# A fused attention and Fourier-mixing kernel on one core: the hand-played order of its first part is replaced, omega's load changes its queue, and the weight loads wait for the first values

## The chip, the cores and the metric

The kernel runs on one core of a Trainium2 chip. A core has TensorE (PE, with its weight loads shown apart as PEld), VectorE (DVE), ScalarE (ACT), GpSimd (POOL) and SyncE (SP); each works through its own instructions in order, and waits on semaphores for the others. The metric is device time in microseconds (us), the median of repeated runs. The profile is of one execution; its times count from the span's start.

## The reference

Two blocks follow each other. The first is attention with random features: batch 8, 8 heads, sequence 576, head size 64, 128 features.

```python
def phi(x):                              # x is q or k, scaled by 64 ** -0.25
    h = x @ omega.T - sum(x * x) / 2
    return exp(h - max(h)) / sqrt(128)
kv, z = phi(k).T @ v, sum(phi(k))        # per batch and head
x = (phi(q) @ kv) / (phi(q) @ z + 1e-6)  # heads side by side: [8, 576, 512]
```

The second mixes with a Fourier transform and ends in a two-layer perceptron:

```python
u = x + real(fft(fft(x, axis=1), axis=2))
un = (u - mean(u)) / sqrt(var(u) + 1e-6)
out = u + max(un @ w_ch1, 0) @ w_ch2     # 512 -> 2048 -> 512
```

The weights w_ch1 and w_ch2 arrive as 64-bit floats; the kernel reads them as pairs of 32-bit words and makes 32-bit floats of them itself.

## The kernel before

**Two parts.** The first part holds all attention, all mixing, the conversion and preparation of the weights, and four "plain" tiles of 128 rows of the perceptron. The second part does the other 4096 rows in eight blocks of 512, with a Strassen-like scheme (lines 1118 on, 1309). Both are written as generators, the streams, that yield a `Step` (engine or engines, length in us, latency, events it waits for, buffers it takes and gives) ahead of the instructions that the step stands for. `Listing` (line 107) plays them against a planner's clock, and the instructions come out in that order, in one queue for each engine.

**What sets the order.** In the second part, `run` always takes the step that can start first. In the first part it doesn't choose: the string `PICKS` (line 48) holds one character for each of its 1819 steps, the place in the list of waiting steps, in base 36. So in the first part the planner's lengths don't set the order. They still set which engine does a step that names two, and which PSUM bank is taken. The constants RATE, HOP and TURN (lines 38 to 41) are the planner's DMA rate, the delay from one engine to another, and the cost of a change of matmul shape.

**The first part, pair by pair.** There are 32 pairs of heads (`attn`, line 512), handled by three streams in turn. For one pair:

- SP loads k and q (lines 347, 350; 288 KB each; two buffers) and v (line 355; three buffers, vd).
- PE transposes k and q in nine 128x128 blocks (line 470), ACT evicts them (line 477, kqT).
- PE makes the scores against omega (line 544, 64x64 corners of the array), DVE takes the maximum of each group (line 488, nmx), ACT makes the exponentials (line 505, e).
- PE sums keys times values (line 578), ACT or DVE keeps the result (lines 592, 594), PE transposes the query features (line 470) and makes numerators and denominators (lines 621, 629). DVE divides (lines 638 to 641) into x.

After four pairs a batch is whole, and `mix` (line 653) follows: DVE and POOL fold x (lines 668 to 694), PE multiplies with cosine and sine tables (lines 712, 739, 744), ACT keeps and DVE and POOL add up (lines 760 to 778), SP stores u to memory.

**The weights.** `weights` (line 422) issues 32 loads of 512 KB on POOL's queue (line 434, raw), with four buffers; each is followed by `narrow` (line 397): a multiplication on ACT or POOL (lines 409, 407), four instructions on DVE (lines 411, 413, 416, 418), and an addition on POOL (line 420). The plain tiles need the converted weights: line 863 transposes a normed tile, line 924 multiplies with w1, line 947 with w2. `w2_parts` (line 998), `weight_sums` (line 1062) and `block_norms` (line 976) prepare the second part.

**The start.** omega (om) is loaded by two DMAs on SP's queue (line 366) ahead of everything else there; PE transposes it (line 449) and DVE scales it (line 451) before the first scores. Each stream of the list waits for events: `weights` begins when the planner has issued the load of vd number 1, an event of the planner alone, with no instruction behind it.

Of the kernel before, what the change touches and what calls it, by code (L numbers as in the profile page):

```python
# [3 lines left out]

# [12 lines left out]
F32 = mybir.dt.float32  # L17
# [20 lines left out]
RATE = 190.0  # L38
HOP = 0.15

TURN = 0.1
# [7 lines left out]
    "00e2ede0ebed3dedebfcdcddfeede3fdfhbi8cdefdebfdgafaggec9hddk0kiij2jejgj7lfffffhcdfffdfcggjehegfi7gjbl"  # L49
    "hbhkjgkkdihfhi7hci7bfiadgkhhjce9didbhhb7gggbfihbbf97acbhbeghefaie8bc7chhhcgfc7cedddh9dd1ccdfif8eggih"  # L50
    "f6g8ejihichdihidfkhfhgjckgigh6eihggiddebd6dcg9eei7cfhei6ddfgihhj78gmkmiidaggjfigdmlg6khhjcj6agghifgg"
    "kh6afejekjkjfigji6j8hjjjiilcj9iegcigdhllkmldjmkkf9j80lca5m7bdai6gfikjaljkika6lhjggic9feikeejhgjij5d7"
    "ldjeafedkdeikjje5g5ielfafej6egkicg8dffgikghjijiee7eeifaaeefhefehdeh7iffd6hb7eeidiedhggiijbkj35fjkjhk"
    "kfgfhkk3h795g4e4i6khchlijigkjji4hlfjfd8lfhlg4mi64bfgjjedjgibk6ijj5cgcijhicgi6lii9fi9lf6ggdijf6bgd8fe"
    "icddchifajihj9fgihgjgi6jbhi6degcbg48ffgfh6ii5kjigihf7jgf9ejggafji7gf7egdfh6ficd6dbhfeeh5addfh5be5bff"
    "c48gai8hg9ageefcj5j7gh6haeeghhjikiehi5mg6lghhl5jjhagd5nglkmlccnjldj9llj45lkjjaemh6gbmlf8f7hgekef6hke"
    "87cldljj8bkhihbhhdc6ffgadkdf7ad5kdbgjhhig6lgcel5mdjedilaidedejihgjegi5ggjhcf5dgc5c775kccdh489j8ddgff"
    "h8cbdgiejkkechjhkkki5gj7kgjjjjfjjjh4i7dhhjjfi4k4h4kjchehg6ihk975g5bfejcehg3dgmggiej6m55bf9igig5h66gg"
    "jjjfiieifh8ege5kdihdlhiheief9k5fimhmcio8hgk7fge5jhgdeifagbgbjeeekhgclgigh7ge8fgefddfaci4icdffhgfid8f"
    "gjffhgihd6gc6cjeelgf3af8hbiccgchgfebg5c9d6ehdfcfeeagghffbhc6f9egchggh6aeehfeekjccbdfafdf50h0gcgabgea"  # L60
    "7fcdcfabg6be8bd4c9dcdcdbcebe6bcgb6cefbacadfeaca7dcdcdchdf9abca66f8dcbd8b98c8aa9c8dd2eabcc87a7b758697"
    "a27277ba9688848aa89a99992b98aa9a287a888729d8a993ba8ac9788aede65bdaacb69ba8ba659b54387a986aaa9baccade"
    "ad9b7bfcecffffde79fe9e6h9bgc3gc3be1eac26e7ebeddbdfeefegd6cdfed2ddf3dadeb3e3cc9dc6c5dbbdcab7b3c72b79b"
    "acbb8abbb679a6a9bb9ab49c7b38a93caa998888888888899888686981458778888888888888841933648786583b59691776"
    "a7c67267761bb4bcb6cc9a679a8aaba3f94df49cbaa675793a9aa88778388a88a93995aa39b94a4954585536126424112222"
    "3333533555523346545266421330442216087635433437704543770334535754155544556455155414437756241426224444"
    "1112032232202111100"
# [39 lines left out]
class Listing:  # L107
# [4 lines left out]
    def __init__(self, buffers):  # L112
        self.free = dict.fromkeys((PE, ACT, DVE, POOL, SP, NONE, PORT), 0.0)
        self.buffers = {name: [0.0] * n for name, n in buffers.items()}
        self.made = {}
        self.moved = 0.0
        self.mode = "whole"
        self.banks = [0.0] * 8
        self.got = None
# [12 lines left out]
    def start(self, step, ready, before):  # L132

        queued = before in step.engines and len(step.engines) == 1
        t = ready[0] if queued else ready[1]
        for ev in step.after:
            if ev not in self.made:
                return None
            t = max(t, self.made[ev])
        for name in set(step.take):  # L140
            if name in WIDTH:
                t = self.banks_at(WIDTH[name], t)[1]
                if t == math.inf:
                    return None
                continue
            free = sorted(self.buffers[name])
            n = step.take.count(name)
            if len(free) < n:
                return None
            t = max(t, free[n - 1])  # L150

        def begin(e):
            return max(t, self.free[e] if e != NONE else 0.0, self.free[PORT] if step.on_port(e) else 0.0)

        eng = min(step.engines, key=lambda e: begin(e) + step.engines[e])
        t = begin(eng)
        return t + (TURN if eng == PE and step.mode != self.mode else 0.0), eng

    def run(self, streams, picks=None):
        todo = []  # L160
        picks = iter(picks or ())

# [14 lines left out]
        while todo:  # L177
# [20 lines left out]
            done = end + step.late + (HOP if eng != NONE else 0.0)  # L198
            if step.kb:
                self.moved = max(self.moved, end) + step.kb / RATE  # L200
                done = max(done, self.moved + 1.6)
# [52 lines left out]
def kernel(  # L254
# [110 lines left out]
    for i in range(2):  # L365
        nc.sync.dma_start(om[:, i, :], omega[:, :])
# [4 lines left out]
    om2 = fix.tile([128, MF], F32, name="om2")  # L371

# [24 lines left out]
    def narrow(i, dst, raw):  # L397


        lo, hi = raw[:, :, 0], raw[:, :, 1]  # L400
        lof, hif, bits = lo.bitcast(F32), hi.bitcast(F32), dst.bitcast(U32)


        step = Step({ACT: 0.72, POOL: 1.4}, after=(("raw", i),), port=True, bias=1.11)
        yield step
        if step.eng == POOL:
            nc.gpsimd.tensor_scalar(dst, hif, 2.0**-112, None, op0=ALU.mult)
        else:
            nc.scalar.activation(out=dst, in_=hif, func=AF.Copy, scale=2.0**-112)
        yield Step(DVE, 0.43, port=True, bias=0.19)  # L410
        nc.vector.tensor_scalar(hi, hi, 0x80000000, None, op0=ALU.bitwise_and)
        yield Step(DVE, 1.15, port=True, bias=0.36)
        nc.vector.scalar_tensor_tensor(
            bits, bits, 3, hi, op0=ALU.logical_shift_left, op1=ALU.bitwise_or
        )
        nc.vector.tensor_scalar(hi, bits, 0xFF800000, None, op0=ALU.bitwise_and)
        yield Step(DVE, 0.7, port=True, bias=-0.99)
        nc.vector.scalar_tensor_tensor(lof, lo, 2.0**-52, hif, op0=ALU.mult, op1=ALU.mult)  # L418
        yield Step(POOL, 1.3, makes=("w", i), give=("slab",), port=True, bias=1.25)
        nc.gpsimd.tensor_tensor(out=dst, in0=dst, in1=lof, op=ALU.add)  # L420

    def weights():
# [3 lines left out]
        yield Step(NONE, after=(("vd", 1),))  # L426
# [17 lines left out]
    def first():  # L444

        yield Step(NONE, 3.0)
        yield Step(PE, 0.4, take=("bank",))
        b, omps = got()
        nc.tensor.transpose(omps[:, 0:128], om[:].rearrange("m i d -> m (i d)"), ident[:])
        yield Step(DVE, 0.3, makes="om2", give=(b,))  # L450
        nc.vector.tensor_scalar(om2[:], omps[:, 0:128], SCALE, None, op0=ALU.mult)

    def transposed(src, name, groups, after, makes, give, back=None):
# [3 lines left out]
        for j0, j1 in groups:  # L457
# [3 lines left out]
                0.11 * m,  # L461
# [12 lines left out]
    def evicted(dst, b, j0, j1, makes, back):  # L474
        yield Step(ACT, 0.15 + 0.115 * (j1 - j0), 0.1, makes=makes + (j0,), give=(b,), bias=0.08)
# [5 lines left out]
    def softmax(n, ts, num, b, es):  # L481
# [3 lines left out]
        yield Step(DVE, 0.15 + 0.27 * num, bias=-0.56)  # L485
# [10 lines left out]
        for i, one in enumerate(b):  # L496
            if num == 4 or not i:
                yield Step(
                    ACT, 1.18 if num == 4 else 0.65, 0.0, take=(size,),
# [12 lines left out]
    def attn(n):  # L512
# [16 lines left out]
        def pairs_of(js, *ts):  # L529
# [4 lines left out]
                0.235 * len(js),  # L534
# [52 lines left out]
        def keep():  # L587
            step = Step({DVE: 0.3, ACT: 0.35}, take=("kv",), give=(kvb,), makes=("kv", n))
# [20 lines left out]
            1.23,  # L609
# [24 lines left out]
        yield Step(DVE, 1.25, after=(("frame", b),), give=(ndb,), makes=("x", b, pr), bias=-0.07)  # L634
# [18 lines left out]
    def mix(b):  # L653
# [7 lines left out]
        def folds(n):  # L661
            op = (ALU.add, ALU.subtract)[n]
            even, odd = (ALU.subtract, ALU.add) if n else (ALU.add, ALU.subtract)
            step = Step({DVE: 1.22, POOL: 2.5} if n else DVE, 1.22, take=("half",), port=True)
# [4 lines left out]
            yield Step(DVE, 1.15, port=True, bias=-0.08)  # L669
# [3 lines left out]
            for dst, src in ((h[:, 0:NL], h[:, 0:NL]), (h[:, NL : NL + 1], x[:, 4:5])):  # L673
# [7 lines left out]
                {DVE: 1.2, POOL: 2.6} if n else DVE, 1.2,  # L681
# [18 lines left out]
        for n, (tab, name) in enumerate(((cs, "cs"), (cs, "cs"), (sn, "sn"), (sn, "sn"))):  # L700
# [19 lines left out]
            def kept(n=n, yb=yb, yp=yp):  # L720
                yield Step(ACT, 0.44, 0.1, makes=("y", b, n), give=(yb,), bias=0.1)
                nc.scalar.activation(out=y[:, n, :], in_=yp[:, 0:NK], func=AF.Copy)

            yield Fork(kept())
        for c in range(NC3):
# [3 lines left out]
                1.33,  # L729
# [23 lines left out]
    def residual(b, c, x, abb):  # L753
# [3 lines left out]
        yield Step(ACT, 0.4, 0.1, take=("bmp",), give=(b1,))  # L757
# [4 lines left out]
        for last, (dst, op) in enumerate(((mi, ALU.subtract), (pl, ALU.add))):  # L762
            yield Step(DVE, 0.67, give=(b0,) if last else (), bias=-0.1)
# [23 lines left out]
        yield Fork(summed(0, mi, pl, DVE, 0.85))  # L787
        if c < NL:
            yield from summed(1, pl, mi, POOL, 1.6)
# [54 lines left out]
    def norm_of(j, t, i, pool, dst):  # L844
# [7 lines left out]
        yield Step(DVE, 1.09, bias=-0.23)  # L852
# [3 lines left out]
        yield Step(POOL, 0.7, port=True, bias=-0.18)  # L856
        nc.gpsimd.tensor_tensor(rstd[:], rstd[:], mhalf[:], op=ALU.pow)  # L857
        yield Step(DVE, 0.56, port=True)
        nc.vector.tensor_scalar(u[:], u[:], mv[:, 0:1], rstd[:], op0=ALU.subtract, op1=ALU.mult)
        yield Step(PE, 0.45, take=("bank",), give=("u",))  # L860
# [5 lines left out]
        yield Step(ACT, 0.6, 0.1, give=(b,), makes=("unT", j, i), bias=0.33)  # L866
# [25 lines left out]
    def plain_of(j):  # L892
# [4 lines left out]
        def hidden(fc, b, hp):  # L897
            step = Step(
                {ACT: 0.15 + TP / 1130.0, DVE: 0.15 + TP / 945.0},
                late=0.1,  # L900
# [12 lines left out]
        for fc in range(NFC):  # L913
            yield Step(
                PE,
                8 * TP / 1193.0,
# [38 lines left out]
    def rest(t, b, yp):  # L955
# [3 lines left out]
        yield Step(DVE, 0.7, after=(("op", t),), give=(b,), bias=1.38)  # L959
# [16 lines left out]
    def block_norms(j, pool):  # L976
# [13 lines left out]
        for i, (o, l, r, op) in enumerate(ops):  # L990
            yield Step(DVE, 0.7, makes=("tt", j) if i == 3 else None, port=True, bias=-0.49)
# [6 lines left out]
    def w2_parts():  # L998
# [14 lines left out]
        def op(o, l, r, **kw):  # L1013
            step = Step({DVE: 0.7, POOL: 1.35}, port=True, **kw, bias=-0.63)
# [47 lines left out]
    def weight_sums(groups):  # L1062
        yield Step(NONE, after=("converted",))
        for g in groups:
# [6 lines left out]
            for i, (o, l, r, op) in enumerate(ops):  # L1071
                yield Step(DVE, 0.7, makes=("w1s", g) if i == 3 else None, port=True)
# [34 lines left out]
    late = ctx.enter_context(tc.tile_pool(name="late", bufs=1))  # L1107
    listing.buffers = {k: [0.0] * n for k, n in dict(
# [338 lines left out]
```

## Time and profile before

| | us |
|---|---|
| median of five runs | 1225.64 |
| lowest and highest | 1223.47 and 1227.53 |
| the profiled execution, its own time | 1224.47 |
| its span in the profile | 1222.6 |
| PE busy | 1188.5 (97%) |
| PEld busy | 1065.0 (87%) |
| DVE busy | 745.8 (61%) |
| ACT busy | 458.0 (37%) |
| POOL busy | 383.3 (31%) |

The page begins with these busy times, then cuts the span into 40 slices of 30.6 us and gives the busy share of each in tenths. Busy time of PE is modelled from pipelined matmuls, so a busy PE may still issue matmuls further apart than it could; start times of successive matmuls tell more. The chain of work follows the last instruction back to what released it, step by step; each of its rows has a start, a length, an engine, a tile, a line and a number of instructions. A row of waits has the engine that waited, the one it waited for, the total, the number of waits and the longest.

The DMA queues moved 206.02 MB, 169 GB/s over the span; in the first 20 us it was 275 GB/s.

### The profile page before, as it was taken

What the parts mean: (1) busy time and instruction counts of PE and PEld (TensorE: products, weight loads), DVE (VectorE), ACT (ScalarE), POOL (GpSimd) and SP (SyncE); (2) the same over time, 40 slices, a digit from 0 to 9 for tenths busy, and PEclk for the clock granted to TensorE, in tenths of its full rate; (3) what the DMA queues carried; (4) which work ended last, traced back from release to release, by engine and by line L of the source; (5) the groups of instructions that cost most, each with busy time, mean ns of one, the idle gap of its engine ahead of it and who ended that gap; (6) DMA issues with size and microseconds to landing.
All of it is one profiled execution on the core that took longest, in us unless ns stands there. A gap on an engine that the chain in (4) does not pass through costs nothing.

```text
span 1222.6 us, 31614 instructions
## 1 busy us (share of the span) xinstructions
PE 1188.5 (97%) x12705; PEld 1065.0 (87%) x12705; DVE 745.8 (61%) x1522; ACT 458.0 (37%) x1432; POOL 383.3 (31%) x451
## 2 busy tenths in 40 slices
PE   6989889999999999999999999999999999999997
PEld 5778878878878777999899899899899899899897
DVE  4899999896674664384384285285276266267255
ACT  6867767666653521222222222222222222222211
POOL 3443443531111013322422421432431531431421
PEclk9999999999999999999999999999999999999999
DMA  9564654636663334195096096186176276268255
GB/s 262 155 209 143 201 176 145 215 93 201 184 193 130 123 113 163 50 308 169 32 305 190 9 305 190 31 285 191 51 260 199 59 248 219 61 210 256 61 175 171
DMA packets 149058, 206.02 MB, mean 169 GB/s; under 512 B 49328, under 2 KB 62896, under 8 KB 148912
## 3 DMA queue, kind: packets, MB, share of 16 engines
q1 hardware_dynamic: 144224, 187.15, 49.1%
q0 software_dynamic: 4608, 16.78, 4.1%
q8 instruction: 101, 1.65, 0.6%
q14 instruction: 45, 0.37, 0.1%
q10 hardware_dynamic: 80, 0.07, 0.0%
HBM read 172.23 MB, written 35.91 MB: 170 GB/s over the span
## 4 chain that ended last, share of the span: by engine, by line
PE 92%; DVE 4%; ACT 2%; issue 1%; DMA 0%; SPq 0%; DVEq 0%; ACTq 0%
PE banks L1130 32%; PE banks L1309 29%; PE banks L924 5%; PE banks L947 5%; PE banks L470 4%; PE banks L544 4%; PE banks L712 4%; PE banks L578 3%; PE banks L621 2%; PE banks L739 2%; ACT e L505 1%; PE banks L863 1%; DVE nmx L488 1%; PE banks L744 1%; ACT kqT L477 1%
## 5 line engine op out<-in xcount | busy, mean ns | idle before, releaser
L1116 DVE CUSTOM_DVE_ANT_0 hid<-banks,s 128x256 f32<-128x256 f32 x192 | 79.7, 423 | 254.9 <-PE banks L1130 254.9
L1309 PE MATMUL banks<-wl,sums 128*128 128x128 f32 x1792 | 220.2, 275 | 0.0
L1309 PEld LDWEIGHTS banks<-wl,sums 128*128 128x128 f32 x1792 | 210.5, 192 | 1.0
L505 ACT ACTIVATE e<-banks,nmx 128x128 f32<-128x128 f32 x576 | 158.9, 397 | 41.0 <-DVE nmx L488 41.0
L1144 ACT ACTIVATE s<-banks 128x256 f32<-128x256 f32 x192 | 73.6, 383 | 257.6 <-PE banks L1130 257.6
L1130 PE MATMUL banks<-unT,w 128*128 128x256 f32 x704 | 167.3, 379 | 0.0
L1130 PEld LDWEIGHTS banks<-unT,w 128*128 128x128 f32 x704 | 132.7, 190 | 17.9 <-issue 0.5
L1284 ACT ACTIVATE s<-banks 128x128 f32<-128x128 f32 x168 | 46.5, 277 | 236.6 <-PE banks L1309 175.3
L1130 PE MATMUL banks<-tt,w1s 128*128 128x256 f32 x512 | 126.3, 379 | 0.0
L1197 POOL TENSOR_TENSOR hs<-hid 128x256 f32<-128x256 f32 x64 | 46.4, 725 | 200.1 <-DVE hid L1116 173.5
L1130 PEld LDWEIGHTS banks<-tt,w1s 128*128 128x128 f32 x512 | 97.2, 190 | 13.3
L488 DVE TENSOR_REDUCE nmx<-banks 128x8 f32<-128x1024 f32 (+1 forms) x96 | 88.3, 952 | 32.2 <-PE banks L544 27.6
L1309 PE MATMUL banks<-wl,hid 128*128 128x128 f32 x768 | 98.8, 275 | 0.0
L1309 PEld LDWEIGHTS banks<-wl,hid 128*128 128x128 f32 x768 | 94.0, 192 | 1.2
L1289 DVE TENSOR_TENSOR part<-banks,s 128x128 f32<-128x128 f32 x168 | 48.6, 289 | 75.3 <-PE banks L1309 74.2
L1197 POOL TENSOR_TENSOR hs<-hid,hs 128x256 f32<-128x256 f32 x64 | 46.4, 726 | 118.7 <-issue 93.3
L1130 PE MATMUL banks<-unT,w1s 128*128 128x256 f32 x320 | 80.6, 379 | 0.0
L544 PE MATMUL banks<-om,kqT 64*64 64x128 f32 x2304 | 77.0, 276 | 3.4 <-ACT kqT L477 2.0
L857 POOL TENSOR_TENSOR rstd<-rstd,mhalf 128x1 f32<-128x1 f32 x36 | 29.0, 806 | 153.2 <-DVE rstd L855 137.4
L544 PEld LDWEIGHTS banks<-om,kqT 64*64 64x64 f32 x2304 | 64.1, 134 | 14.6 <-ACT kqT L477 4.6
L1309 PE MATMUL banks<-wl,hs 128*128 128x128 f32 x576 | 74.9, 275 | 0.4 <-DVE part L1289 0.4
L420 POOL TENSOR_TENSOR w<-w,raw 128x512 f32<-128x512 f32 x32 | 43.8, 1367 | 99.0 <-DVE raw L418 79.2
(115 smaller groups left out, 1998.6 us busy)
## 6 DMA issues: line engine op xcount, KB each, us to landing
wl<-w2l SPq DMA_DIRECT2D x392, 256.0 KB, 3.6
raw<-in_moe_w_ch_dram POOLq DMA_DIRECT2D x32, 512.0 KB, 5.0
kq<-in_k_dram SPq DMA_DIRECT2D x32, 288.0 KB, 4.4
kq<-in_q_dram SPq DMA_DIRECT2D x32, 288.0 KB, 4.3
vd<-in_v_dram SPq DMA_DIRECT2D x32, 288.0 KB, 4.6
out_dram<-ur SPq DMA_DIRECT2D x68, 128.0 KB, 2.4
u<-us SPq DMA_DIRECT2D x32, 256.0 KB, 4.0
ur<-us SPq DMA_DIRECT2D x32, 256.0 KB, 3.5
```

The source lines that it names most:

```text
L470: nc.tensor.transpose(ps[:, (j - j0) * 128 : (j - j0 + 1) * 128], src(j), ident[:])
L488: nc.vector.tensor_reduce(nmx[:, :, 0:num], pps[:, :, 0 : MF * num].rearrange("p b (c m) -> p b c m", m=MF), axis=AX.X, op=ALU.max, negate ...
L505: nc.scalar.activation(out=e[:, c + (i if num == 1 else 0), :], in_=pps[:, i, MF * c : MF * c + MF], func=AF.Exp, bias=nmx[:, i, c : c + 1],)
L544: nc.tensor.matmul(pps[cols, c, MF * m : MF * m + MF], lhsT=kqT[rows, j, cols], rhs=om2[rows, :],)
L712: nc.tensor.matmul(yp[:, 0:NK], lhsT=fold[:, c, n, :], rhs=tab[:, c, :], start=(c == 0), stop=(c == NC3 - 1),)
L924: nc.tensor.matmul(hp[:, 0:TP], lhsT=w1[:, dc, 128 * fc : 128 * fc + 128], rhs=unTs[key][:, dc, :], start=(dc == 0), stop=(dc == NDC - 1),)
L947: nc.tensor.matmul(yp[:, 0:DM], lhsT=hs[fc][:, 128 * i : 128 * i + 128], rhs=w2[:, fc, :], start=(fc == 0), stop=(fc == NFC - 1),)
L1116: nc.vector._custom_dve(TENSOR_ADD_SAT, out=o, in0=ps, in1=sb, s0=FMAX, s1=0.0)
L1130: nc.tensor.matmul(ps[:, 0:HT], lhsT=left(dc), rhs=right(dc), start=start and dc == 0, stop=(dc == D2 - 1), skip_group_check=True,)
L1144: nc.scalar.activation(out=s[:], in_=ps[:, 0:HT], func=AF.Copy)
L1197: nc.gpsimd.tensor_tensor(out=o, in0=l, in1=r, op=op)
L1309: nc.tensor.matmul(ps[:, 0:128], lhsT=left[:, f], rhs=wls[j, i, n][:, f], start=start and f == 0, stop=(f == 3), skip_group_check=True,)
```

## The change

- **Planner.** The constants move into a tuple `Clock`, one for each part. The first part's clock has another DMA rate and hop, a `lead` ahead of PE's steps, a `tail` of latency for each engine, a `lag` after PE, and a list of engines on which a stream's next step may follow in the queue without waiting for the end. The second part's clock has the old constants, empty tails and lags, and all engines in that list.
- **Step lengths** of the first part are set anew, some 30 of them.
- **PICKS** is replaced as a whole; it has 1819 characters as before.
- **omega** is loaded on ACT's queue instead of SP's.
- **Gate.** `weights` begins with a copy of one element of vd0 on POOL, which waits until v of the first pair has landed; the weight loads stand behind it in POOL's queue.

The diff, cut: of PICKS the first line, of the step lengths those that the text speaks of.

```diff
-RATE = 190.0
-HOP = 0.15
-
-TURN = 0.1
+class Clock(NamedTuple):
+    rate: float
+    hop: float
+    lead: float
+    turn: float
+    tail: dict
+    lag: dict
+    queues: tuple
+
+
+FIRST = Clock(
+    270.0, 0.036, 0.2, 0.12, {PE: 0.163, ACT: 0.105, DVE: 0.085, POOL: 0.02}, {DVE: 0.12, ACT: 0.055},
+    (PE, SP, NONE),
+)
+SECOND = Clock(190.0, 0.15, 0.0, 0.1, {}, {}, (PE, ACT, DVE, POOL, SP, NONE))
...
 PICKS = (
-    "00e2ede0ebed3dedebfcdcddfeede3fdfhbi8cdefdebfdgafaggec9hddk0kiij2jejgj7lfffffhcdfffdfcggjehegfi7gjbl"
...
+    "00ed01eaaeda3eeefbgeddeege9h3hhhhhbggciajkcfdalaabgallekffjkkji3iigeh0iiiidhh7ggggcffdfcffghgbiefhe8"
...
     def __init__(self, buffers):
+        self.clock = FIRST
...
     def start(self, step, ready, before):
 
+        clock = self.clock
         queued = before in step.engines and len(step.engines) == 1
-        t = ready[0] if queued else ready[1]
+        queued = queued and (before in clock.queues or step.kb > 0)
+        t = 0.0 if queued else ready[1]
...
+        if PE in step.engines:
+            t += clock.lead
+        if queued:
+            t = max(t, ready[0])
+
         def begin(e):
-            return max(t, self.free[e] if e != NONE else 0.0, self.free[PORT] if step.on_port(e) else 0.0)
+            u = ready[1] + clock.lag.get(e, 0.0) if before == PE and not queued else 0.0
+            return max(t, u, self.free[e] if e != NONE else 0.0, self.free[PORT] if step.on_port(e) else 0.0)
...
-            done = end + step.late + (HOP if eng != NONE else 0.0)
+            done = end + step.late + clock.tail.get(eng, 0.0) + (clock.hop if eng != NONE else 0.0)
             if step.kb:
-                self.moved = max(self.moved, end) + step.kb / RATE
+                self.moved = max(self.moved, end) + step.kb / clock.rate
...
     for i in range(2):
-        nc.sync.dma_start(om[:, i, :], omega[:, :])
+        nc.scalar.dma_start(om[:, i, :], omega[:, :])
...
+    gate = fix.tile([1, 1], F32, name="gate")
...
-        step = Step({ACT: 0.72, POOL: 1.4}, after=(("raw", i),), port=True, bias=1.11)
+        step = Step({ACT: 0.57, POOL: 1.55}, after=(("raw", i),), port=True, bias=1.11)
...
-        yield Step(DVE, 0.43, port=True, bias=0.19)
+        yield Step(DVE, 0.34, port=True, bias=0.19)
...
-        yield Step(DVE, 1.15, port=True, bias=0.36)
+        yield Step(DVE, 1.19, port=True, bias=0.36)
...
-        yield Step(DVE, 0.7, port=True, bias=-0.99)
+        yield Step(DVE, 0.61, port=True, bias=-0.99)
...
-        yield Step(NONE, after=(("vd", 1),))
+        yield Step(POOL, 0.1, after=(("vd", 0),))
+        nc.gpsimd.tensor_copy(out=gate[:], in_=vds[0][0:1, 0, 0:1])
...
-        yield Step(ACT, 0.15 + 0.115 * (j1 - j0), 0.1, makes=makes + (j0,), give=(b,), bias=0.08)
+        yield Step(ACT, 0.05 + 0.107 * (j1 - j0), 0.02, makes=makes + (j0,), give=(b,), bias=0.08)
...
-        yield Step(DVE, 0.15 + 0.27 * num, bias=-0.56)
+        yield Step(DVE, 0.063 + 0.267 * num, bias=-0.56)
...
-                    ACT, 1.18 if num == 4 else 0.65, 0.0, take=(size,),
+                    ACT, 1.0 if num == 4 else 0.5, 0.04, take=(size,),
...
-            step = Step({DVE: 1.22, POOL: 2.5} if n else DVE, 1.22, take=("half",), port=True)
+            step = Step({DVE: 1.13, POOL: 2.5} if n else DVE, 1.13, take=("half",), port=True)
...
-                {ACT: 0.15 + TP / 1130.0, DVE: 0.15 + TP / 945.0},
-                late=0.1,
+                {ACT: 0.165, DVE: 0.2},
...
     late = ctx.enter_context(tc.tile_pool(name="late", bufs=1))
+    listing.clock = SECOND
```

## The prediction

> **What bounds the kernel now.** I read the page's slices first, then the busy times by stretch, the chain of work, the waits and the groups by shape. The slices (30.6 us each) say where time can be won at all:
>
> ```profile
> PE   6989889999999999999999999999999999999997
> ...
> DVE  4899999896674664384384285285276266267255
> ```
>
> PE is at 9 from the seventh slice on; the low digits are at the left, where DVE stands at 8 and 9. The second part begins at 464.6 us (first matmul of line 1130). In the trace its matmuls follow each other every 216 ns (line 1130) and 112 ns (line 1309), and the 95th percentile of both spacings is the same as the median: nothing to win behind 464.6 us. So the question is the first part. By stretches (PE, PEld, DVE, ACT, POOL busy, clock, DMA):
>
> ```profile
> 0.00:20.00 20.00, 11.01 (x244) 9.52 (x245) 5.61 (x8) 10.46 (x33) 9.23 (x18) 1.00 0.91 275
> 20.00:60.00 40.00, 36.40 (x839) 30.12 (x839) 33.62 (x59) 34.47 (x116) 12.56 (x11) 1.00 0.69 181
> 60.00:100.00 40.00, 34.61 (x850) 31.24 (x850) 35.44 (x70) 28.23 (x89) 18.04 (x19) 0.96 0.66 194
> ...
> 180.00:220.00 40.00, 39.80 (x785) 34.70 (x784) 37.60 (x75) 30.06 (x99) 17.29 (x17) 0.96 0.48 154
> ...
> 300.00:340.00 40.00, 40.00 (x723) 36.23 (x720) 24.76 (x54) 26.83 (x89) 6.98 (x8) 1.00 0.57 166
> ```
>
> To 300 us DVE is busy 85 to 94%, afterwards 62% or less, with PE full. Busy PE is not dense PE, so I price the PE work itself, from rows of the chain where a step is followed at once by the next:
>
> ```profile
> 360.67 3.63 PE banks L947 x8
> ...
> 371.20 7.14 PE banks L924 x64
> 378.35 3.23 PE banks L712 x12
> ...
> 397.20 1.21 PE banks L578 x72
> 398.41 1.97 PE banks L544 x72
> ...
> 418.92 1.08 PE banks L621 x32
> 420.00 0.23 PE banks L629 x8
> ```
>
> Per pair of heads: 1.97 + 1.21 + 1.31 (lines 621, 629) + 18 transposes of line 470 in 2.02 = 6.51; 32 pairs are 208.3 us. Per batch: two line 712 rows, 6.46, and lines 739/744, 4.3; eight are 86. Per plain tile: two 7.14 rows and 32 matmuls of line 947 at 0.43 (the 1.72 us rows of four), 28.0; four are 112. Transposes of line 863: 8 x 0.44 = 3.5. **Floor 410 us, against 464.6**: 54.8 us of loss, of which 11.7 fall into 0 to 20 us, 36.0 into 20 to 240, 3.9 into 240 to 300, 3.2 into 300 to 420 (each stretch's length less the floor of the matmuls in it). In 20 to 240 it is waits on in-order queues; PE's and ACT's (total us, times, longest):
>
> ```profile
> PE banks L470 <- ACT e L505: 5.3, 6, 1.9
> PE banks L578 <- ACT e L505: 2.8, 4, 1.3
> PE banks L621 <- ACT e L505: 2.0, 1, 2.0
> ```
>
> ```profile
> ACT e L505 <- DVE nmx L488: 16.0, 16, 1.9
> ```
>
> PE waits for the exponentials (line 505), which wait for DVE's maxima (line 488), which stand in DVE's queue behind conversions and mixing. The profiled execution took 1224.47 us, 1.87 more than its span and 1.17 under the median 1225.64; I add 1.17 at the end.
>
> **The change, part by part.** 1. *Step lengths.* The picks are played, so the lengths set no order; they set which engine takes a step that allows two (conversion lines 407/409, kv, folds, relu, line 1017) and which PSUM bank. Old against new against the trace: exponentials of four 1.18, 1.0, 1.15 (a chain row of four); eviction of four 0.61, 0.478, 0.61; maxima 1.23, 1.131 plus a tail of 0.085, 1.22. The new lengths are the engine's issue time with the latency split off, and the sum is what the trace shows. One group is planned shorter than it runs: the conversion on DVE, 2.28 before, 2.14 after, against 0.509 + 0.822 + 0.590 + 0.703 = 2.62 in the trace.
>
> 2. *Start.* om's two loads leave SP's queue, so the first k load issues at 0.73 instead of 1.65 us. The four raw loads (2 MB, issued 1.38 to 4.1 us) leave the way of kq and vd. The first transpose now waits for kq until 6.90 us. A kq load lands 4.4 us after issue by the page's median, so 5.1 us; not above 275 GB/s, 288 KB cannot take under 1.1 us, so not before 1.9 us. PE's first step wants om: 4.16 us now; if it queues behind ACT's table load (1.28 us) it lands 1.28 later, 5.4, and its transpose of 0.44 ends at 5.9. Bounds of the gain: 6.90 - 5.9 = 1.0 and 6.90 - 4.6 = 2.3; I take 1.8, nearest to the kq row. PE's first transposes run slowly there (nine in 2.18 us at 6.90, nine in 1.20 at 13.22); that moves along and is neither gain nor loss. Following the first thirty picks by hand, the queue is k, q, vd, then the next k, q, and the gate; PE's first three steps of scores keep their order, so the exponentials hold PE at 9 to 13 us as before: nothing more is booked.
>
> 3. *The gate.* One 1x1 copy on POOL waits for vd0 (now landing 11.2 us after its issue at 3.60). Its own time: between 0.10 (a 128x1 memset) and 0.71 us (line 857's power on 128x1); 0.1 taken, in idle POOL (9.2 of 20 us busy). Behind it on POOL stand all raw loads and line 407. vd0 lands after 4.6 us (page) to 11.2 us from an issue near 1.7, so the first raw load issues at 6.3 to 12.9 instead of 1.38 and lands 5 us later, 11.3 to 17.9; four conversions of 1.53 follow. DVE first touches raw (line 411) at 27.8 us, so 4 to 10 us of cover remain: cost 0. Without that cover it is 32 conversions that start late, but they are spread to 200 us: at most the delay itself, 5 to 11 us, once. SP, moved past by om alone, is free earlier; ACT's queue has two issues of about 0.45 us before its first eviction at 8.05: hidden.
>
> 4. *The order.* Bounds from the stretches. Nothing gained: 0. If 20 to 240 us ran like 240 to 300 (3.9 in 60, 1.3 per 20): 36.0 - 14.3 = 21.7 us. DVE is busy 89% of 20 to 240, and full cover would need 99%, so it can come only by moving DVE work to 300 to 420 us, where DVE is busy 62%. Half, 11, is taken: of the waits above 0.3 us between PE's steps (28 us from 20 us on) a part is of this kind, a part DVE's own load. What is late next is DVE's maxima again, then ACT.
>
> 5. *Second part.* Its clock holds the old constants, and with them each new branch of start() gives the old answer. What differs is only the times at which the first part leaves the engines. The hand-over at 464.6 us has no wait now; DVE is busy 27.4 of the last 44.6 us, so a first part shorter by 13 still fits its weight sums and norms: 0.
>
> Sum: -1.8 - 11 = -12.8; 1224.47 - 12.8 + 1.17 = **1212.8 us**.
>
> [...] The rows say the clock ran at 0.96 in 60 to 100 and in 180 to 220 us: in each, 3.4 us at half speed, 1.7 us of work lost, although no gap between PE's steps there is over 2.6 us. [...] By the rows, dips stand only in the loose stretch, and a denser one could be spared both, 3.4 us; I book none. On om, the rows give 0.92 us of SP time. [...]
>
> **The rivals.**
> - *Start alone* (0.10): the order brings nothing since DVE's 89% is the limit, and one late wait replaces another. 1225.64 - 1.8 = 1223.8, within 0.2%, which is what a measurement of this kernel can tell from no change. For: DVE's digits. Against: DVE has 38% free after 300 us.
> - *More than forecast* (0.15): the whole 21.7, the start's 2.3 and both dips, 27.4: 1198.
> - *Less than forecast* (0.10): the start and 3 us of the order: 1221.
> - *Slower* (0.17): DVE becomes the bound. Its conversions are planned 0.48 us short each, 32 x 0.48 = 15.4 us; with a tighter order these stand before maxima in DVE's queue, in 20 to 240 us, each maximum then holds ACT and PE. It decides once DVE passes about 19 of 20 us there. If PE pays half, and the order gains nothing: +7.7 - 1.8 = +5.9, 1231.5; all of it, 1239. For: POOL and DVE on the conversion slow each other (line 416 takes 0.43 us alone and 1.43 beside line 420 at 77.2 us). Against: the old order carries a shortfall of 0.34 each already.
> - That the change doesn't do what it says is open only for "order kept"; part 5 gives it 0.
>
> **How the numbers follow.** Forecast as worked out 0.48 (1206 to 1220), the rivals 0.15, 0.10 (faster), 0.10 (same), 0.17 (slower). Faster by over 0.2%: 0.48 + 0.15 + 0.10 = 0.73; same 0.10; slower 0.17. The range takes in 1199 (most of the better rival) and 1231 (half of the slower one), leaving out about 2 in 10.
>
> **What would show it.** Right: line 1130 begins at 450 to 455 us; the first transpose at 4.6 to 5.9; raw's first issue between 6 and 13; PE's waits for line 505 in 20 to 240 us halved; DVE over 62% after 300 us; line 1130's spacing still 216 ns. Wrong: DVE over 95% in 20 to 240 us with PE below 36 of 40; the second part longer than 758 us; PE waiting at line 924 for converted weights.

## The result, and the profile after

The changed kernel takes 1228.94 us (median of 25 runs, 1224.96 to 1234.15), the kernel before 1225.57 in the same comparison (49 runs). The ratio is 1.0028 [1.0020, 1.0036]: **slower by 3.4 us**, where 12.8 less was forecast. The profiled execution of the changed kernel took 1229.93 us, with a span of 1228.1. New lines stand about 24 lower in the code: 470 is now 494, 477 501, 488 512, 505 529, 544 568, 578 602, 621 645, 924 947, 1130 1154.

First the timeline of PE in the changed kernel at both ends of the first part (start, duration, instruction, in brackets the idle time before it):

```profile
4.89 0.45 PE L473 MATMUL banks<-ident,om 128*128 128x128 f32 x1 [4.89 <-DMA om<-in_omega_dram]
5.13 2.13 PE L494 MATMUL banks<-ident,kq 128*128 128x128 f32 x9
...
470.20 1.03 PE L1154 MATMUL banks<-unT,w 128*128 128x256 f32 x4
```

The first transpose is 1.77 us earlier (5.13 for 6.90), and yet the second part begins 5.6 us later (470.20 for 464.57). From there to the end it is 757.9 us, before 758.0. So all of the loss lies between 5 and 470 us. The slices and the stretches (columns as before):

```profile
PE   7989989999999999999999999999999999999997
...
DVE  5897978898776433274284285275275266266255
```

```profile
0.00:20.00 20.00, 13.48 (x292) 12.02 (x295) 7.18 (x10) 12.15 (x39) 4.87 (x16) 1.00 0.84 256
20.00:60.00 40.00, 36.32 (x902) 31.57 (x898) 33.22 (x61) 36.26 (x121) 11.96 (x11) 0.96 0.73 205
60.00:100.00 40.00, 34.21 (x739) 30.75 (x732) 34.55 (x67) 28.34 (x93) 16.93 (x18) 0.96 0.60 178
...
180.00:220.00 40.00, 35.53 (x696) 30.80 (x690) 32.93 (x66) 28.65 (x93) 15.27 (x17) 0.96 0.51 151
220.00:260.00 40.00, 38.08 (x863) 32.83 (x854) 35.48 (x68) 32.66 (x110) 13.75 (x13) 0.96 0.63 192
...
300.00:340.00 40.00, 39.28 (x799) 31.80 (x799) 29.16 (x64) 28.11 (x90) 10.40 (x9) 1.00 0.80 252
```

In 180 to 220 us PE is busy 35.5 instead of 39.8, and DVE isn't the reason: it too is less busy, 32.9 for 37.6. Four stretches stand at clock 0.96 instead of two. What PE waits for in 20 to 240 us (us in total, times, longest), and below it ACT:

```profile
PE banks L568 <- issue: 3.5, 2, 2.1
PE banks L494 <- ACT e L529: 3.4, 4, 1.6
PE banks L602 <- issue: 3.2, 3, 2.7
PE banks L494 <- DVE x L665: 2.5, 1, 2.5
PE banks L602 <- ACT e L529: 2.3, 3, 1.3
...
PE banks L645 <- DVE kv L616: 1.8, 1, 1.8
```

```profile
ACT e L529 <- DVE nmx L512: 21.6, 15, 5.7
```

The waits for the exponentials (line 529, before 505) did fall, from 10.5 to 6.1 us, small rows included. Two single waits for DVE came in, 2.5 and 1.8. All rows with a named engine make 16.6 before and 12.9 after: 3.7 won in this stretch. Behind it, from 240 us to the second part, the new order has named waits of 3.2 us, where the kernel before has none; the two largest rows:

```profile
PE banks L736 <- DVE fold L711: 1.6, 1, 1.6
PE banks L494 <- ACT e L529: 1.0, 2, 0.6
```

So over both stretches only some 0.5 us of named waits are won. But 6.7 us now stand at **"issue"** in 20 to 240 us: PE waited for nothing that the profile shows. In the kernel before, this row is missing from 20 to 240 us. The chain of work names the places (start, us, what):

```profile
181.62 1.42 issue
183.03 1.54 PE banks L568 x48
184.57 1.28 PE banks L494 x9
185.85 1.20 PE banks L602 x70
187.06 2.69 issue
189.74 0.33 PE banks L602 x2
```

PE stops after 16 of 64 and after 70 of 72 matmuls of one kind, in the middle of a step, and the profile shows no semaphore that it waits for. Over the whole first part such gaps ("gaps at issue"; here and below those over 0.25 us, from 10 us on) make 6.88 us (at 89.6, 94.7, 183.0, 189.7 and 324.0); before it is one of 0.62. The page's lines on instructions and on DMA queues give a reason to think of:

```profile
PE 1191.3 (97%) x12705; PEld 1069.8 (87%) x12705; DVE 729.0 (59%) x1512; ACT 457.1 (37%) x1445; POOL 370.7 (30%) x449
...
q8 instruction: 101, 1.65, 0.6%
```

Queue q8 carries 101 packets of 16 KB, and PE has 25,410 recorded instructions: 252 to a packet, about 256 with those that its sequencer handles (25,835 in all). So a packet is a block of PE's own program. In the trace the packets that bear on the three large gaps begin at 92.30, 180.58 and 187.31 us; PE goes on at 94.66, 183.03 and 189.74, each time 2.4 us later. Between these points stand 13 times 256 and once 256 instructions: PE goes on with the first one of the block that was fetched. Counted from there, PE had 0, 32 and 0 instructions left when the three packets began. In the kernel before it never had under 59 from 20 us on, and the median packet of either kernel begins with some 190 to 200 left. The packet itself is not slow: 0.95, 0.92 and 0.97 us at the three, 1.0 in the median. It begins late: 2.7, 2.4 and 4.3 us after PE took up the block in hand, against a median of 1.1 in this kernel and 0.8 in the one before. The stretches of these three delays, and the gap behind the third:

```profile
89.56:92.30 2.74, 2.74 (x128) 2.74 (x128) 1.19 (x3) 2.33 (x10) 2.74 (x3) 1.00 0.98 326
178.20:180.58 2.38, 2.38 (x113) 2.13 (x112) 1.20 (x3) 1.79 (x5) 1.14 (x1) 1.00 0.76 248
183.03:187.31 4.28, 4.03 (x127) 3.38 (x127) 3.41 (x5) 3.40 (x13) 0.29 (x1) 1.00 0.87 236
187.30:189.80 2.50, 0.06 (x1) 0.06 (x2) 2.40 (x5) 0.36 (x1) 0.00 (x0) 1.00 0.93 329
```

While the packets are awaited, the DMA engines are 76 to 98% busy; in the last row PE stands still for 2.5 us. The theory **starved PE** follows: loads crowded together make the fetch of PE's next instruction block begin late. From 20 us on no packet begins with more than 299 instructions left (296 in the kernel before), so in these two traces PE's program came no further ahead of PE than that.

Accounting for the 5.6 us of the two profiled executions: start -1.8, gaps at issue +6.3, two more spells of half clock (four for two) +3.4 (1.7 each, an estimate: 3.41 us at half speed), and -2.3 left. The order's named waits give some 0.5 of that; the rest has no place in the profile. Over all runs the clock is kinder: its mean is 0.9945 (26 runs) against 0.9958 (35 runs of before in the first comparison below; 0.9956 to 0.9965 in the others), 0.0013 x 1228 = 1.6 us, one spell more on average.

Gaps, waits and begins below are read from one execution of each kernel; in order_alone, after_straight, gate_alone, after_spaced and before_double it was the slowest on record, in before_straight and before_grouped the fastest.

### The profile page after: what moved, and what is told of

It is laid out like the page before. It is cut to its first block, busy times and chain, and to the rows that moved or that the text cites. A ratio compares the mean times of both kernels' runs of the same rounds, so it can differ in the third digit from the quotient of the medians.

```text
span 1228.1 us, 31615 instructions
## 1 busy us (share of the span) xinstructions
PE 1191.3 (97%) x12705; PEld 1069.8 (87%) x12705; DVE 729.0 (59%) x1512; ACT 457.1 (37%) x1445; POOL 370.7 (30%) x449
## 3 DMA queue, kind: packets, MB, share of 16 engines
q8 instruction: 101, 1.65, 0.6%
## 4 chain that ended last, share of the span: by engine, by line
PE 91%; DVE 4%; ACT 3%; issue 1%; DMA 0%; ACTq 0%; DVEq 0%
PE banks L1154 32%; PE banks L1333 29%; PE banks L947 5%; PE banks L494 5%; PE banks L970 5%; PE banks L568 4%; PE banks L736 4%; PE banks L602 3%; ACT e L529 2%; PE banks L645 2%; PE banks L887 1%; DVE nmx L512 1%; PE banks L763 1%; DVE x L801 1%; PE banks L768 1%
## 5 line engine op out<-in xcount | busy, mean ns | idle before, releaser
L1333 PE MATMUL banks<-wl,sums 128*128 128x128 f32 x1792 | 216.8, 275 | 0.0
L568 PEld LDWEIGHTS banks<-om,kqT 64*64 64x64 f32 x2304 | 67.5, 139 | 17.2 <-issue 6.6
L1333 PEld LDWEIGHTS banks<-wl,hs 128*128 128x128 f32 x576 | 70.5, 192 | 0.9 <-DVE part L1313 0.6
```

The lines of the kernel that those rows point to most:

```text
L568: nc.tensor.matmul(pps[cols, c, MF * m : MF * m + MF], lhsT=kqT[rows, j, cols], rhs=om2[rows, :],)
L1333: nc.tensor.matmul(ps[:, 0:128], lhsT=left[:, f], rhs=wls[j, i, n][:, f], start=start and f == 0, stop=(f == 3), skip_group_check=True,)
```

## The experiments

Rivals to "starved PE": **the order itself** (one late wait replaced by another; the loads don't matter), **density** (PE uses up a block faster than the next can come, loads or not), and **the copies** (a 512 KB copy with reversed rows in memory, behind which SP's next k load takes 4.5 to 5.3 us to issue, at 84.1 and 180.9 us, just before the gaps). Figures for "before" are of the same comparison.

**start_alone**: the kernel before with omega's queue and the gate, and the old order.

```diff
-        nc.sync.dma_start(om[:, i, :], omega[:, :])
+        nc.scalar.dma_start(om[:, i, :], omega[:, :])
...
-        yield Step(NONE, after=(("vd", 1),))
+        yield Step(POOL, 0.1, after=(("vd", 1),))
+        nc.gpsimd.tensor_copy(out=gate[:], in_=vds[0][0:1, 0, 0:1])
```

> The kernel before with the changed start only: omega loaded on ACT's queue and the one-element copy ahead of the weight loads; old order, old step lengths. The prediction's parts 2 and 3 say 1.8 us faster than before (1.0 to 2.3), first transpose at 4.6 to 5.9 us. A rival says that the start is swallowed by the next wait on the exponentials at 9 to 13 us, and later by the conversions: 0 to 0.5 us.

1223.19 against 1225.64 us, ratio 0.9981 [0.9969, 0.9992]. Its first transposes, then its 60 to 100 and 180 to 220 us:

```profile
5.79 2.13 PE L472 MATMUL banks<-ident,kq 128*128 128x128 f32 x9
```

```profile
60.00:100.00 40.00, 34.00 (x859) 30.45 (x858) 35.97 (x70) 28.91 (x91) 18.07 (x19) 1.00 0.67 197
...
180.00:220.00 40.00, 39.26 (x792) 33.96 (x791) 38.16 (x76) 30.73 (x101) 18.47 (x17) 1.00 0.49 155
```

The start is worth its price: 2.3 us by the ratio, 1.0 to 3.8 by its interval. Of the kernels here that compute the reference's values it is the only one clearly faster than both.

**order_alone**: the changed kernel without the other two.

```diff
-        nc.scalar.dma_start(om[:, i, :], omega[:, :])
+        nc.sync.dma_start(om[:, i, :], omega[:, :])
...
-        yield Step(POOL, 0.1, after=(("vd", 0),))
-        nc.gpsimd.tensor_copy(out=gate[:], in_=vds[0][0:1, 0, 0:1])
+        yield Step(NONE, after=(("vd", 0),))
```

> The changed kernel with the old start: omega on SP's queue, no copy ahead of the weight loads; new order and lengths. If the order alone is what lost, this is slower than the kernel before by the measured 3.4 us plus the start's gain, about 5 us. If the held-back weight loads cost something, it is faster than the changed kernel, under 3 us over before.

1229.23 against 1225.64, ratio 1.0029 [1.0017, 1.0040]. The loss comes with the order, and holding the weight loads back isn't what costs. But it is 3.6 us and not the 5 that adding up would need: the changed kernel, with the start, has 1.0028, so the start's gain doesn't show there. Gaps at issue are 8.2 us in its profiled execution, which took 1238.68 us, 9.5 over the median; I take no other size from it.

**after_straight** and **before_straight**: each kernel with its copies made straight, rows not reversed.

```diff
-                us[b][nh : 2 * nh, :].rearrange("t (i d) -> i t d", i=4),
-                uh[b][nh - 1 :: -1, :].rearrange("t (i d) -> i t d", i=4),
+                us[b][nh : 2 * nh, :],
+                uh[b][0:nh, :],
```

> The changed kernel in which the eight copies of 512 KB from memory to memory no longer reverse the rows and move whole rows of 2 KB instead of pieces of 512 B; the rows therefore land in another order than the reference asks for. Theory F, instructions: PE runs out of instructions because their 16 KB blocks come late while such a copy and the loads queued behind it hold the DMA queues; then PE's gaps that nothing releases fall from 6.9 us to under 2 and the time falls by 3 to 6 us, to before or below. Theory W, waits: the new order has as many waits on DVE and ACT as the old one, and the copies do not matter: within 1 us of the changed kernel.

> The kernel before with the same straight copies (rows in another order than the reference). Theory F: little to gain, since PE has 0.6 us of gaps that nothing releases: 0 to 1.5 us faster. Theory W: the same as in the changed kernel, within 1 us.

1229.20 and 1224.73 against 1225.64: 1.0027 [1.0016, 1.0038] and 0.9999 [0.9986, 1.0012]. SP's long issues at 84 and 181 us are gone from after_straight, and the gaps stay at their places, 8.1 us in all. The rival of the copies falls.

**after_noraw**: the changed kernel with the first four weight loads only, whose buffers are used again.

```diff
+    raws = []
...
-                raw = slabs.tile([128, CV, 2], U32, name="raw", tag="slab")
-                nc.gpsimd.dma_start(raw[:].rearrange("p n two -> p (n two)"), src.bitcast(U32))
+                if i < 4:
+                    raw = slabs.tile([128, CV, 2], U32, name="raw", tag="slab")
+                    nc.gpsimd.dma_start(raw[:].rearrange("p n two -> p (n two)"), src.bitcast(U32))
+                    raws.append(raw)
+                raw = raws[i % 4]
```

> The changed kernel with only the first four weight loads; the other 28 (512 KB each) are left out and the conversions read the four buffers again, so the converted weights are not the reference's. Straight copies had left PE's gaps without a releaser where they were, so theory F in its first form, the copies, has fallen. Theory F2, crowded loads: PE's next 16 KB of instructions come late wherever several loads of k, q, v or weights are issued within 4 us. Then the gaps at 181 to 190 us, which have two weight loads beside them, vanish, and the gap at 92 to 95 us, which has seven loads of k, q and v and no weights, stays at about 2 us; the time falls by 3 to 6 us. Theory D, density: a block of 256 PE instructions is simply used up faster than the next can come; then all the gaps stay within 1 us of 6.9 and the time moves by less than 1 us.

1222.37 against 1225.07, ratio 0.9986 [0.9972, 0.9999], where the changed kernel has 1.0028: 0.42%, or 5.1 us, won. PE's waits in 20 to 240 us:

```profile
PE banks L573 <- issue: 2.5, 2, 1.3
```

Gaps at issue are 3.2 us in all, less than half. It is not quite the pattern that was expected: of the two gaps at 181 to 190 us the large one (2.7) is gone and the first (1.4) is still 1.15, and the one at 94.7 us, with no weight load near, fell from 2.1 to 1.3.

**after_noloads** and **before_noloads**: straight copies, the weight loads as in after_noraw, and of k, q and v only the loads that fill each buffer once.

```diff
+            if n < NKQ:
+                kq = ld.tile([P, 2 * R, D], F32, name="kq", tag="kq")
+                nc.sync.dma_start(kq[:, 0:R, :], k[b, h].rearrange(rows, r=R))
+                kept_kq.append(kq)
+            kq = kept_kq[n % NKQ]
...
```

> The changed kernel with the straight copies and with nearly all loads of the first part left out: k and q after the first two pairs, v after the first three, weights after the first four; the buffers are read again, so the values are not the reference's. F2: no late block is left, PE's gaps without a releaser fall below 1 us in all, the clock drops at most twice, and the time falls by 6 to 10 us, to 1219 to 1223. D: the gaps stay at 5 us or more.

> The kernel before with the same loads left out and the straight copies (values not the reference's). Its PE has 0.6 us of such gaps, so F2 and D both expect little: 0 to 2 us faster. What is left between this and after_noloads is then the order alone, without instructions and loads: the prediction's part 4 says 11 us for the changed order, theory W (as many waits on DVE and ACT as before) says 0 to 3.

1219.67 and 1222.30 against 1225.07: 0.9959 [0.9944, 0.9974] and 0.9981 [0.9971, 0.9991]. Without loads the changed kernel is the faster one, by 2.6 us with the start in it. By the ratios the loads cost the changed kernel 8.5 us (1.0028 - 0.9959) and the kernel before 2.3 (1 - 0.9981): the difference of 6.2 (some 2.4 either way by the intervals) is what turned the gain into a loss, and it is near the size of the gaps, which fall from 6.9 to 1.0 us in the one, and from 0.6 to 0 in the other. Density falls with it: the order is the same, and from 20 us on no packet of after_noloads begins with fewer than 108 instructions left. PE's waits in 20 to 240 us of after_noloads:

```profile
PE banks L505 <- ACT e L540: 5.4, 5, 2.6
PE banks L613 <- ACT e L540: 2.3, 3, 1.3
...
PE banks L656 <- DVE kv L627: 1.8, 1, 1.8
PE banks L505 <- DVE x L676: 1.4, 1, 1.4
PE banks L656 <- issue: 1.0, 1, 1.0
```

With named engines it is 13.7 us, 16.6 in before_noloads. But behind 240 us the new order has its 3.2 us of named waits here too, and the old one none: 16.9 for 16.6, nothing won. The waits for DVE and ACT don't shrink without the loads either (13.7, with them 12.9), so the loads act on PE's instructions and not on these. By time the changed kernel is 2.6 us ahead, and its first scores begin 1.4 us earlier (7.57 for 9.01). So of the forecast 11 some 1 is left to the order, which the intervals don't tell from nothing.

**gate_alone**: start_alone with omega left on SP.

```diff
-        yield Step(NONE, after=(("vd", 1),))
+        yield Step(POOL, 0.1, after=(("vd", 1),))
+        nc.gpsimd.tensor_copy(out=gate[:], in_=vds[0][0:1, 0, 0:1])
```

> The kernel before with only the one-element copy ahead of the weight loads; omega stays on SP's queue. If the held-back weight loads make the start's gain, nearly the 2.3 us of start_alone: 1.3 to 2.3. If the queue of omega makes it: 0 to 0.9.

1225.64 against 1225.07, ratio 1.0003 [0.9991, 1.0015]: no change, although the first scores begin at 7.43 us instead of 9.01. The held loads, issued at 9.8 to 11.6 us, were followed by a gap of 2.41 us at issue at 19.9, which would take that back; in start_alone it is 0.73 us there.

**om_alone**: start_alone without the gate (the first pair of lines of its diff).

> The kernel before with omega's two loads on ACT's queue and nothing else of the change. start_alone (both parts) was 2.45 us faster than before in its call, gate_alone 0. If omega's queue alone makes that gain (k is issued 0.9 us earlier and PE starts earlier): 1.5 to 2.5 us faster than before, first transpose near 6. If both parts are needed (k early, and the first weight loads out of its way): 0 to 1 us faster, the first transpose at 6.3 or later.

1223.98 against 1226.46, ratio 0.9992 [0.9978, 1.0006]; first scores at 7.31 us. The medians say 2.5 us, the interval reaches to no change: inconclusive.

**after_spaced**: a weight load directly behind another goes out after POOL's next operation, or before the conversion that needs it.

```diff
+            if eng == POOL and not step.kb:
+                self.loaded = bool(self.held)
+                if self.held:
+                    self.held.pop(0)[1]()
...
+        while any(n == i for n, _ in listing.held):
+            listing.held.pop(0)[1]()
...
+                if i >= 4 and listing.loaded:
+                    listing.held.append((i, load))
+                else:
+                    load()
+                    listing.loaded = True
...
```

> The changed kernel, but a weight load that stood directly behind another on POOL's queue goes out only after POOL's next operation. Theory 'starved PE' (loads issued close together make PE's own instruction blocks late): the gaps of PE that nothing releases fall from 6.9 us to 3 to 5, and the time by 1 to 3 us against the changed kernel. Rival 'the order itself' (waits on DVE and ACT): gaps and time as in the changed kernel, within 1 us.

1228.99 against 1226.46, ratio 1.0019 [1.0006, 1.0032]. Gaps at issue: 7.8 us. The expectation failed, and the run tells little: the pair before the largest gap stayed a pair (183.7 and 184.3 us), since a conversion that needs the second one follows at once in the order. The changed kernel's gap at 94.7 us had no weight load within 5 us before it at all. Pairs on POOL's queue alone are not the point; after_noraw and after_noloads say that the loads of weights and of k, q and v both count.

**before_grouped**: the reverse, in the kernel before.

```diff
+                if i >= 4 and i % 2 == 0:
+                    listing.held.append((i, load))
+                else:
+                    while listing.held:
+                        listing.held.pop(0)[1]()
+                    load()
...
```

> The kernel before, but its weight loads from the fifth on go out in pairs, the earlier one of a pair held back until the later one is due. Theory 'starved PE': gaps of PE that nothing releases appear (1 to 4 us; the kernel before has 0.6), and the time is 0 to 3 us above the kernel before. Rival 'the order itself': no such gaps, and the same time within 1 us, unless a conversion comes too late for its load, which would show as a wait for raw.

1230.30 against 1226.46, ratio 1.0034 [1.0021, 1.0048], but gaps at issue of 1.1 us only, in a profiled execution of 1227.01 us. It is slower, and not by what the theory names in that execution; why stays open.

**before_double**: the kernel before with the weight loads' traffic doubled.

```diff
+                if i >= 4:
+                    spare = dram.tile([128, 1024], U32, name=f"spare{i}")
+                    nc.gpsimd.dma_start(spare, src.bitcast(U32))
```

> The kernel before, but each weight load from the fifth on is followed on POOL's queue by a second transfer of the same 512 KB into a spare piece of memory that nothing reads: the traffic of the weight loads is doubled, and the order, the engines' work and the results stay. Theory 'starved PE' (crowded transfers make PE's own instruction blocks late): gaps of PE that nothing releases grow from 0.6 to 4 us or more, each ending some 2.4 us after the start of a packet of the instruction queue, and the time is 5 to 15 us above the kernel before. Rival (the old order is safe from it, or crowding only delays the loads themselves): those gaps stay under 1.5 us, and what time is lost stands as PE's waits for k, q, v or raw and what hangs on them.

1230.34 against 1224.62, ratio 1.0046 [1.0033, 1.0059]. PE's waits in 20 to 240 us, then one gap in the timeline and the stretch that it fills:

```profile
PE banks L547 <- issue: 2.4, 2, 2.1
PE banks L581 <- issue: 1.9, 3, 1.0
...
PE banks L624 <- issue: 0.7, 1, 0.7
```

```profile
54.91 1.32 PE L547 MATMUL banks<-om,kqT 64*64 64x128 f32 x40 [2.07 <-issue]
```

```profile
52.40:54.90 2.50, 0.43 (x12) 0.19 (x4) 1.06 (x3) 1.45 (x6) 1.35 (x1) 1.00 0.96 255
```

Gaps at issue grow from 0.6 to 5.4 us (this execution took 1233.67 us), with the order unchanged. The block's packet begins at 52.42 us, 5.1 us after PE took up the block before, with 6 instructions in hand; PE goes on 2.5 later, with the DMA engines 96% busy. The largest others end 2.3 to 2.5 us after a packet's begin as well. The expectation held, in the gaps and in the time (5.7 us by the medians). In this run more transfers alone, in the old order, starved PE.

## Why the prediction was wrong, step by step

- **Floor and loss** (410 us, 36.0 of loss in 20 to 240): the sums come out, and they held the trap. Loss that could be won by order was put at 0 to 21.7 with half taken. That bound is more than all of PE's idle time there, 17.2 us (before, then after; PE's busy time is the first number behind the length, DVE's the third):

```profile
20.00:240.00 220.00, 202.78 (x4246) 175.13 (x4244) 197.48 (x385) 162.07 (x523) 89.98 (x85) 0.98 0.60 180
20.00:240.00 220.00, 200.26 (x4315) 176.25 (x4310) 188.63 (x380) 165.78 (x544) 81.36 (x81) 0.97 0.61 182
```

  **This step failed**, the order's 11 us: some 0.5 us of named waits were won with the loads, none without them, and of the time without loads some 1 us. A late maximum, quotient or kv in DVE's queue took the place of the late exponential (2.5 and 1.8 us in two single waits), ACT's waits for the maxima rose from 16.0 to 21.6, and behind 240 us 3.2 us of waits came in. Two readings beside it were off and bear nothing: DVE is at 78% in 340 to 380 us (31.33 of 40), not 62 or less, and the page's slices reach 308 GB/s, so 275 was no ceiling.
- **What the step left out**: a bound below nothing. The row "issue" stood in the profile before (0.6 us), and the instruction queue stood on the page; neither was priced. A new order of the same work is a new order of the transfers too, against PE's own program. That was +6.3 us in the profiled pair. That 1228.94 lies between 1199 and 1231 is luck: the range reached so far for a slower rival with another mechanism.
- **Start** (-1.8, first transpose at 4.6 to 5.9): right in size where it stands alone, with a poor sign. The first transpose is at 5.13, but in the six profiled executions with the old start it scatters from 5.17 to 6.90. The first scores (line 544, now 568) are steadier: 8.6 to 9.1 us with the old start, 7.2 to 7.8 in the eight with omega's queue or the gate or both. start_alone is 2.45 us faster by medians, but in the new order the start's gain doesn't show (order_alone 1.0029, with the start 1.0028). That the raw loads have to leave the way of kq for it, as part 2 of the prediction has it, the trace doesn't bear out: om_alone has its first scores at 7.31 without the gate. Which of the two parts makes start_alone's gain stays open.
- **Gate** (0, raw's first issue at 6.3 to 12.9): right. Issue at 6.29, the copy itself 0.18 us; gate_alone 1.0003.
- **Second part** (0): right, 757.9 for 758.0.
- **Slower by a DVE bound** (0.17): right sign, wrong mechanism. DVE passed 19 of 20 us in three stretches (60 to 80, 140 to 160, 200 to 220: 19.1 to 19.2), before in one (200 to 220: 19.2), and PE was busy 17.4, 19.4 and 20.0 in them; the large gaps lie elsewhere. Over 20 to 240 us DVE is less busy than before, and the four conversion instructions got shorter, not longer, 2.28 us for 2.62:

```profile
L441 DVE SCALAR_TENSOR_TENSOR raw<-raw 128x512 f32<-128x512 uint32 x32 | 22.3, 696 | 1.1
L436 DVE SCALAR_TENSOR_TENSOR w<-w,raw 128x512 uint32<-128x512 uint32 x32 | 22.1, 690 | 0.7
L434 DVE TENSOR_SCALAR raw<-raw 128x512 uint32<-128x512 uint32 x32 | 14.7, 464 | 1.6 <-POOL w L430 1.2 <-ACT w L432 0.4
L439 DVE TENSOR_SCALAR raw<-w 128x512 uint32<-128x512 uint32 x32 | 13.7, 429 | 1.1
```

  The third number is the mean in ns: 464 + 690 + 429 + 696. What the new lengths planned (2.14) was nearer than the rival took it to be.
- **The clock** (none booked): it went the other way, by one spell of 1.7 us on average. From 10 us on, the profiled execution of the changed kernel has four drops, with no gap of PE over 2.7 us; that of the kernel before has two, with none over 2.0.
- **The signs named beforehand**: line 1154 at 450 to 455 us failed (470.2). The waits for the exponentials came near to halving (6.1 for 10.5) and did not help: in after_noloads, where the gaps at issue are 1.0 us for 6.9, these waits are 8.1, so while PE stands still for its instructions the exponentials seem to catch up. DVE in 300 to 340 us at 73% was no sign either: 300 to 460 us together have 92.3 us of DVE, 102.2 before. Of the signs for "wrong" none came: DVE is at 86% in 20 to 240 us, the second part takes 757.9 us, and line 947 (before 924) waits for no weights. No sign named PE's own instructions.

## What to carry to other kernels

Price a new order by what it does to the transfers as well as to the engines: here PE's 25,410 recorded instructions came in 101 packets of 16 KB on a DMA queue, and without most of the loads (after_noloads) the gaps at issue fell from 6.9 us to 1.0. Look for gaps put down to "issue" in the middle of a step, and lay the packets of the instruction queue beside them. When most of a gain is an estimate between nothing and a bound, ask also what could make that term negative, and take the small sure part (here the start) by itself.

## What the runs showed of the hardware

- PE's program arrived in blocks of 16 KB, 256 instructions (101 packets for 25,835 instructions; 256 between the gaps at 183.03 and 189.74 us). A block's packet took 0.97 us in the median of the changed kernel (0.99 before), and at the three large gaps PE went on 2.4 us after its begin, whether the DMA engines were 66% busy meanwhile (180.58 to 183.03 us) or 95% (187.31 to 189.74). What the loads moved is the packet's begin: with 0 to 32 instructions left by then PE stood still for 1.4 to 2.7 us in the changed kernel, and without the loads (after_noloads) no packet from 20 us on began with fewer than 108. No single number of instructions decides: in the kernel before 105 left still gave a gap of 0.62 us (287.87), and 59 none (30.34).
- In the two profiled executions, before and after, from 10 to 1210 us, every drop of the clock lasted 3.41 us and went to half, and the stretches at full clock between two drops are whole multiples of that: 61.44, 92.16 and 30.72 us (18, 27 and 9 times) in the changed kernel, 92.16 before. In windows of 3.41 us counted on and back from the drops, the clock fell after all four in which PE had been idle for 1.89 us or more, after two of the five with 1.65 to 1.81 us, and after none with less. The profiled execution of before has two drops (mean clock 0.996), that of start_alone, with the same order, none (0.999). The changed kernel has four gaps of 1.8 us or more, before two, and a wider spread of its times (9.2 us over 25 runs, before 6.1 over 49).
